# Nyström attention and two dense layers: heads paired by parity, landmark products as eight 64x32 tiles, second-layer blocks of 512, 512, 512, 384 and 384 tokens

## The chip, the cores and the metric

The kernel runs on one core of one Trainium2 chip. The metric is device time in microseconds (us), here the median of three timed runs. One further execution was recorded by the hardware profiler; all rows below come from it. The engines are PE (TensorE, matrix products; PEld is its weight load), DVE (VectorE), ACT (ScalarE), POOL (GpSimd) and SP (SyncE, which here issues the DMAs). Products accumulate in PSUM, which has eight banks of 128 partitions by 512 fp32 values.

## The reference

Attention with 32 landmarks a head (4 batches, 8 heads, 576 positions, head size 64), then two dense layers over the 2304 resulting tokens of width 512. Everything is fp32.

```python
# per batch and head; m = 32, S = 576, D = 64
q_lm, k_lm = means of q, k over S // m = 18 consecutive positions
A  = softmax(q @ k_lm.T / 8)      # 576 x 32
Bm = softmax(q_lm @ k_lm.T / 8)   # 32 x 32
C  = softmax(q_lm @ k.T / 8)      # 32 x 576
Z  = Bm.T / (norm1(Bm) * norminf(Bm) + 1e-6)
for _ in range(6): Z = 2 * Z - Z @ Bm @ Z
x = (A @ Z @ C @ v), heads side by side          # 2304 x 512
# layer 1: 512 -> 2048 -> 512
h = x @ moe_w_in;  y = (h * sigmoid(h)) @ moe_w_out
# layer 2: 512 -> 2048 -> 512
h = y @ moe2_w_in; out = (h * tanh(softplus(h))) @ moe2_w_out
```

## The kernel before

**Attention without x.** The kernel never forms x. For each batch it makes W = Z·C·v (32 landmarks by 64 values for each head) and multiplies it with the rows of the first layer's input weights that belong to the head: u = Wᵀ·w_in. Then h = uᵀ·Aᵀ, where Aᵀ lies with all 8 heads' landmarks on the partitions (`ath`, two groups of 128). Four heads make a unit (b, g), g = 0 or 1. W of a unit goes from a PSUM bank `wk` into a tile `wt`, block diagonal by a mask `own2`, so that one product with 128 rows serves two heads. `u_steps` (L518 to L549) makes u for a batch and a pair `jp` of the 16 column chunks of the hidden layer: eight fp32 matmuls of 128 rows by 64 columns of weights with 128 moving columns, all into one bank; each fp32 matmul runs as two instructions. There are 4 batches by 8 pairs, so 32 such groups. For batch 0 an ACT copy takes the bank to SBUF (L541). For the other batches ACT rounds it to a high part (L546) and DVE subtracts that for a low part (L548), and h is then three products (high·high, high·low, low·high) at L608, as are y and the second layer's `hh`.

**Layer 1.** Tokens go in blocks of 288. A step is one block and one of 16 chunks j of the hidden layer: 6 matmuls for h, SiLU on DVE, ACT and POOL, 12 matmuls for y. y goes to DRAM (`ysc`). Batches 0 and 1 begin in a prelude, in which a planner orders the streams of work (loads, transposes, landmark products, Newton steps, u, h) by listed costs and start delays; `ya` (L829) is batch 0's fp32 y. From then on a loop over steps runs, with the attention of the batch after next worked in between (`bg`). Attention and u of that loop share PSUM banks 5 and 7. In the last block of layer 1 the second layer's weights and inputs come in: each `w2r` tile is loaded by DMA and split in a high part on ACT (`wi2h`, `wh`, L602) and a low part on DVE or POOL (L603).

**Layer 2.** It is written in a fixed order by hand. `NB2` = 384 tokens make a block, 6 blocks, and 16 chunks j each, so 96 steps. A step is 12 matmuls for `hh` (L608, 384 columns each), mish on DVE and ACT over 128x384 tiles (L1025 to L1039), a low part on POOL (L1042), and, two steps later (`LAG2`), 9 matmuls into three banks `o` (L1098, 512 columns each). When a block's last step is accumulated, `out_block` (L1057) copies its three banks through ACT into `ot` tiles (three buffers, L1061) and SP issues the output DMAs (L1069). The `o` banks are five, taken by turns; `hh` has three.

Of the kernel before, what the change touches and what calls it, by code (L numbers as in the profile page):

```python
# [25 lines left out]
NB2 = 384  # L26
# [6 lines left out]
WASTE = 1.33  # L33
# [57 lines left out]
def nystrom_moe_kernel(ctx, tc, q, k, v, w1i, w1o, w2i, w2o, out):  # L91
# [32 lines left out]
    own2 = cp.tile([P, 2], F32, name="own2")  # L124
    blk = cp.tile([P, P], F32, name="blk")
    two = cp.tile([P, 1], F32, name="two")
    for t in (mask2, mask4, sel2, own2, blk):
        pool.memset(t, 0.0)
    pool.memset(two, 2.0)
    for h2 in range(2):  # L130
        pool.memset(mask2[64 * h2 : 64 * h2 + 64, h2 : h2 + 1], 1.0 / (G * 8.0))
        pool.memset(own2[64 * h2 : 64 * h2 + 64, h2 : h2 + 1], 1.0)
# [46 lines left out]
    def load_part(st, nm, p):  # L179
# [3 lines left out]
        h0 = 4 * g + 2 * p  # L183
        if nm != "v" and b in dve_tr:

            t = ap.tile([P, S // M, M], F32, tag=tag, bufs=2, name=f"{nm}{b}{g}{p}")
            for hf in range(2):
                for h2 in range(2):
                    for dh in range(2):
# [4 lines left out]
                            src[b, h0 + h2, hf * HB : (hf + 1) * HB, M * dh : M * dh + M].rearrange(  # L194
# [3 lines left out]
        else:  # L198
# [3 lines left out]
            for h2 in range(2):  # L202
                sp.dma_start(
                    t[:, h2] if apart else t[:, :, h2, :], src[b, h0 + h2].rearrange("(p c) d -> p c d", c=NC)
                )
# [205 lines left out]
    def attn_newton(bt):  # L411
# [27 lines left out]
        for i in range(n):  # L439
            for h2 in range(2):  # L440
                pe.matmul(wk[64 * h2 : 64 * h2 + 64, i, :P], rv[:, i, w:], bt["bb", i], start=True, stop=True)
        yield Step([("dve", 0.3)], (), ("wt", b, gs[-1]))
        for i, g in enumerate(gs):
            pl, tag = (wp, f"gt{g + 1}") if b == 0 else (ap, f"wt{g}")
            wt = pl.tile([P, 2, 2, M], F32, tag=tag, name=f"wt{b}{g}")
            dve.tensor_tensor(
                wt,
                wk[:, i, :P].rearrange("a (p h m) -> a p h m", p=2, h=2),
                own2[:, None, :, None].to_broadcast([P, 2, 2, M]),
                op=ALU.mult,  # L450
            )
            units[b, g]["wt"] = wt
# [65 lines left out]
    def u_steps(b, jp):  # L518

        deps = [("wt", b, 0), ("wt", b, 1)]  # L520
        if b == 0:
            deps += [("wc", 2 * jp), ("wc", 2 * jp + 1), ("ath", 0, 1)] + ([("u", 0, jp - 2)] if jp > 1 else [])
        elif b == 1:
            deps += [("y", 1, 2 * jp + 1)] + ([("u", 1, jp - 2)] if jp > 1 else [])
        yield Step([("pe", 0.9)], deps)
        ub = atbank(f"u{b}{jp}").rearrange("a (j g f) -> a j g f", j=2, g=2)
        for g in range(2):
            wt = units[b, g]["wt"]
            for jj in range(2):
                for p in range(2):  # L530
                    pe.matmul(  # L531
                        ub[64 * p : 64 * p + 64, jj, g],
                        wt[:, p].rearrange("a h m -> a (h m)"),
                        wc[2 * jp + jj][:, (2 * g + p) * P : (2 * g + p + 1) * P],
                        start=True,
                        stop=True,
                    )
        if b == 0:
            yield Step([("act", 0.6)], (), ("u", 0, jp))
            uw[jp] = wp.tile([P, 2, 2, P], F32, tag=f"u{jp}", name=f"uf{jp}")  # L540
            act.copy(uw[jp], ub)  # L541
            return
        yield Step([("act", 0.6)])
# [3 lines left out]
        yield Step([("dve", 0.7)], (), ("u", b, jp))  # L547
        dve.tensor_tensor(ul, ub, uh.bitcast(F32), op=ALU.subtract)  # L548
# [61 lines left out]
    wc = {}  # L610
    wout = {}

# [13 lines left out]
    def h0_matmuls(hb, j, hf):  # L626
        for g in range(2):
            pe.matmul(hb[:, :HB], uw[j // 2][:, j % 2, g], ath[0][:, g, hf * HB : (hf + 1) * HB], start=g == 0, stop=g == 1)  # L628

    def h1_matmuls(hb, b, j, hf):  # L630
        uh, ul = uw[j // 2]
        sl = slice(hf * HB, (hf + 1) * HB)
        for g in range(2):
            wh, wl = uh[:, j % 2, g], ul[:, j % 2, g]
# [213 lines left out]
    streams += [(head_load(*it), Banks(), 1.31) for it in order]  # L848
    streams += [(first_unit(0, 0), Banks(0, 1, 2), 0.38), (first_unit(0, 1), Banks(3, 4, 5), 0.05)]
    for g in range(2):  # L850
        streams += [(queries(units[0, g]), q01, (0.32, 0.25)[g])]
        for ti in range(2):
            streams += [(attn_transposes(units[0, g], ti, 3 * g + ti), Banks(), (1.35, 0.06)[g])]
    streams += [(u_steps(0, jp), Banks(6 + jp % 2), 0.38 + 0.05 * jp) for jp in range(NF // 2)]
    streams += [(h_stream(j, hf), Banks(), 0.59 + 0.01 * (2 * j + hf)) for j in range(NF) for hf in range(2)]
    streams += [(win_stream(j), Banks(), 1.08 + 0 * j) for j in range(NF)]
    streams += [(y_stream(), Banks(), 1.18)]
    streams += [(wout_stream(j), Banks(), 1.17 + 0.05 * j) for j in range(NF)]
    for g in range(2):
        streams += [(attn_transposes(units[1, g], ti, 4 + ti), Banks(), (0.75, 0.87)[g]) for ti in range(2)]  # L860
        streams += [(second_attention(g), a1, (0.67, 1.15)[g])]
        streams += [(attn_softmax(units[1, g]), a1, (1.36, 0.66)[g])]
    streams += [(u_steps(1, jp), Banks((3, 4)[jp % 2]), 1.24) for jp in range(NF // 2)]
    streams += [(wsplit_stream(j), Banks(), 2.0) for j in range(NF)]
# [302 lines left out]
```

## Time and profile before

| what | value |
|---|---|
| median of three runs | 896.05 us (895.35 to 901.98) |
| the profiled execution, its own time | 899.86 us |
| its span in the profile | 898.1 us |
| busy share of the span: PE / DVE / ACT / POOL | 96% / 73% / 53% / 33% |
| share of PE in the chain that ended last | 79% |
| PE busy in 0 to 100 us, 100 to 200, 300 to 400, 400 to 500 | 86.07, 96.22, 93.33, 95.69 us |
| PE busy in 200 to 300, 600 to 700, 700 to 800 us | 100.00 us each |

The prelude takes about the first 198 us, layer 1 lasts until about 487 us, layer 2 to the end. The profiled execution took 1.8 us more than its span shows and lies 3.8 us above the median. In a profile row "idle before, releaser" is how long the engine stood still just before the instruction and what set it free. Matmuls are pipelined: the spacing of their starts, not their durations, says what each costs. The granted TensorE clock (PEclk) is a share of full speed: 1.00 is 2.4 GHz and 0.50 is 1.2 GHz.

### The profile page before, as it was taken

How to read it: one execution, taken by the hardware profiler on the slowest of the kernel's cores; microseconds unless marked ns; L12 is line 12 of the kernel's file. 1: busy time of each engine (PE TensorE's matmuls, PEld its weight loads, DVE VectorE, ACT ScalarE, POOL GpSimd, SP SyncE). 2: the span in 40 equal slices, each digit the busy share in tenths (PEclk: the TensorE clock that was granted, in tenths of full speed). 3: DMA queues.
4: the chain of work that ended last, by engine and by line, in shares of the span. 5: the costliest groups of instructions: out<-in, count | busy, mean ns of one | idle time of the engine just before them, and what ended most of it. 6: DMA issues, size and time to landing. Idle time of an engine off the chain costs nothing.

```text
span 898.1 us, 15048 instructions
## 1 busy us (share of the span) xinstructions
PE 863.3 (96%) x5440; PEld 762.3 (85%) x5440; DVE 651.1 (73%) x1265; ACT 472.7 (53%) x1013; POOL 293.9 (33%) x334
## 2 busy tenths in 40 slices
PE   7799989999999998899999999999999999999997
PEld 5567767779998998899899889899999999999896
DVE  3878858676576968742364997787787787797776
ACT  3656546345344646653564555554554554555544
POOL 2211333015343545532433542242242242242221
PEclk8899989999999999999999999999999999999999
DMA  8645663433454576720562210110110110000000
GB/s 230 169 97 169 189 192 101 81 81 88 100 149 101 143 224 222 244 87 17 161 181 68 79 45 1 36 35 1 36 36 1 37 36 1 35 1 1 36 1 35
DMA packets 95354, 79.62 MB, mean 89 GB/s; under 512 B 52528, under 2 KB 80688, under 8 KB 95280
## 3 DMA queue, kind: packets, MB, share of 16 engines
q1 hardware_dynamic: 95280, 78.67, 30.6%
q8 instruction: 42, 0.69, 0.3%
q14 instruction: 32, 0.26, 0.1%
HBM read 60.82 MB, written 17.83 MB: 88 GB/s over the span
## 4 chain that ended last, share of the span: by engine, by line
PE 79%; DVE 8%; DMA 5%; ACT 3%; POOL 2%; issue 2%; SPq 1%; ACTq 0%; DVEq 0%; POOLq 0%
PE hh L608 21%; PE o L1098 20%; PE y L608 14%; PE h L608 7%; PE ya L829 5%; PE u L531 4%; PE ha L628 3%; DMA q<-in_q_dram 2%; PE nw L423 1%; DVE z L1036 1%; DMA w2r<-w2c 1%; DMA k<-in_k_dram 1%; PE cv L374 1%; POOL rawt L590 1%; PE c L307 1%
## 5 line engine op out<-in xcount | busy, mean ns | idle before, releaser
L1042 POOL TENSOR_TENSOR g<-z,g 128x384 fp32r<-128x384 f32 x94 | 96.0, 1022 | 256.0 <-ACT g L1039 253.6
L608 PE MATMUL y<-g,wh 128*128 128x288 f32 x768 | 162.4, 302 | 6.8 <-ACT g L659 2.9
L1098 PE MATMUL o<-wh,g 128*128 128x512 f32 x576 | 165.7, 395 | 2.9 <-ACT g L1039 1.9
L660 POOL TENSOR_TENSOR g<-g,g 128x288 fp32r<-128x288 f32 x96 | 82.4, 858 | 184.9 <-ACT g L659 143.0
L608 PEld LDWEIGHTS y<-g,wh 128*128 128x128 f32 x768 | 124.5, 190 | 12.0 <-ACT g L659 3.1
L608 PE MATMUL hh<-yl,wi2h 128*128 128x384 f32 x384 | 129.6, 337 | 0.0
L608 PE MATMUL hh<-yh,wi2h 128*128 128x384 f32 x384 | 129.2, 336 | 0.0
L608 PE MATMUL hh<-yh,wi2l 128*128 128x384 f32 x384 | 129.1, 336 | 0.0
L1098 PEld LDWEIGHTS o<-wh,g 128*128 128x128 f32 x576 | 106.0, 188 | 23.3 <-ACT g L1039 4.1
L1039 ACT CAST g<-z 128x384 fp32r<-128x384 f32 x96 | 49.3, 514 | 133.6 <-DVE z L1038 133.6
L608 PE MATMUL y<-g,wl 128*128 128x288 f32 x384 | 114.6, 298 | 0.0
L1025 DVE TENSOR_SCALAR e<-hh 128x384 f32<-128x384 f32 x96 | 53.5, 557 | 64.2 <-PE hh L608 63.9
L608 PE MATMUL h<-ath,uw 128*128 128x288 f32 x384 | 95.1, 302 | 0.0
L658 DVE SCALAR_TENSOR_TENSOR g<-th,h 128x288 f32<-128x288 f32 x96 | 43.0, 447 | 55.8 <-ACT th L657 54.3
L1098 PE MATMUL o<-wl,g 128*128 128x512 f32 x288 | 81.7, 391 | 0.0
L1026 ACT ACTIVATE e<-e 128x384 f32<-128x384 f32 x96 | 50.4, 525 | 51.4 <-DVE e L1025 51.2
L608 PEld LDWEIGHTS hh<-yl,wi2h 128*128 128x128 f32 x384 | 72.1, 188 | 3.7
L608 PEld LDWEIGHTS hh<-yh,wi2h 128*128 128x128 f32 x384 | 72.1, 188 | 3.7
L608 PEld LDWEIGHTS y<-g,wl 128*128 128x128 f32 x384 | 73.0, 190 | 0.0
L1036 DVE SCALAR_TENSOR_TENSOR z<-z,r 128x384 f32<-128x384 f32 x96 | 70.0, 729 | 3.3
L608 PEld LDWEIGHTS hh<-yh,wi2l 128*128 128x128 f32 x384 | 72.1, 188 | 0.0
L608 PEld LDWEIGHTS h<-ath,uw 128*128 128x128 f32 x384 | 68.1, 191 | 3.6 <-issue 3.0
(165 smaller groups left out, 1631.7 us busy)
## 6 DMA issues: line engine op xcount, KB each, us to landing
rawi<-in_moe_w_in_dram SPq DMA_DIRECT2D x16, 512.0 KB, 5.6
rawo<-in_moe_w_out_dram SPq DMA_DIRECT2D x16, 512.0 KB, 3.6
rawt<-in_moe_w_in_dram SPq DMA_DIRECT2D x16, 512.0 KB, 4.7
w2c<-ct SPq DMA_DIRECT2D x32, 256.0 KB, 2.6
rawt<-in_moe_w_out_dram SPq DMA_DIRECT2D x16, 512.0 KB, 3.8
w2r<-w2c SPq DMA_DIRECT2D x32, 256.0 KB, 2.8
v<-in_v_dram SPq DMA_DIRECT2D x32, 144.0 KB, 3.1
ysc<-yo SPq DMA_DIRECT2D x32, 144.0 KB, 1.9
```

What stands on the lines that cost most here:

```text
L531: pe.matmul(ub[64 * p : 64 * p + 64, jj, g], wt[:, p].rearrange("a h m -> a (h m)"), wc[2 * jp + jj][:, (2 * g + p) * P : (2 * g + p + 1) ...
L608: pe.matmul(o, a, b_, start=first and i == 0, stop=last and i == n - 1)
L628: pe.matmul(hb[:, :HB], uw[j // 2][:, j % 2, g], ath[0][:, g, hf * HB : (hf + 1) * HB], start=g == 0, stop=g == 1)
L658: dve.scalar_tensor_tensor(g2, th, 1.0, hb[:, :HB], op0=ALU.add, op1=ALU.mult)
L660: eng.tensor_tensor(gl, g2, gh.bitcast(F32), op=ALU.subtract)
L829: pe.matmul(yb[hf, m][:, :HB], wof[j][:, m * P : (m + 1) * P], gst[j // 2][:, j % 2, hf], start=j == 0, stop=j == NF - 1,)
L1025: dve.tensor_scalar(e, h, 20.0, None, op0=ALU.min)
L1026: ins = act.activation(e, e, AF.Exp)
L1036: dve.scalar_tensor_tensor(z, z, -2.0, r, op0=ALU.add, op1=ALU.mult)
L1039: act.copy(gh, z)
L1042: eng.tensor_tensor(gl, z, gh.bitcast(F32), op=ALU.subtract)
L1098: pe.matmul(obank[i][c], a[:, c * P : (c + 1) * P], w, start=j == 0 and k == 0, stop=j == NF - 1 and k == 2,)
```

## The change

**Heads.** A unit g now holds the heads 2(2p + h2) + g, the even or the odd ones. W of unit g lies only in partitions 64g to 64g + 63 of its `wt` ([128, 4, 32]), as a plain copy; the mask is gone, and `wk` is one matmul a unit instead of two. u for a pair jp is again eight matmuls, but of 64 rows by 32 columns of weights with 256 moving columns, and it fills half of two banks, one for each unit. So ACT makes two copies of 128x256 where it made one of 128x512, and DVE two subtractions of 128x256. Each u takes two banks: in the prelude 6 and 7 (batch 0), or 3 and 7 and 4 and 5 by turns (batch 1), in the layer-1 loop both 5 and 7. Batch 0's u(jp) now waits for u(jp-1) where it waited for u(jp-2).

**Blocks.** Layer 2 has five blocks, three of 512 tokens with four output chunks and two of 384 with three, so 80 steps: 48 with 12 `hh` matmuls and 12 `o` matmuls of 512 columns each, and 32 as before. `ot` has two buffers instead of three. The low parts of the second layer's input weights for j >= 2 take SBUF that holds u of batch 3 (tags g0 to g6), so they wait for its last h matmuls; j < 2 have tiles of their own.

**Order of the prelude.** Start delays and costs of the planner's streams are other numbers (ten lines such as the one shown), and `WASTE`, a factor on its time, is 1.14 instead of 1.33.

```diff
-NB2 = 384
+NB2 = (512, 512, 512, 384, 384)
@@ first_unit: W into wt
-        for i in range(n):
-            for h2 in range(2):
-                pe.matmul(wk[64 * h2 : 64 * h2 + 64, i, :P], rv[:, i, w:], bt["bb", i], start=True, stop=True)
+        for i, g in enumerate(gs):
+            pe.matmul(wk[64 * g : 64 * g + 64, i, :P], rv[:, i, w:], bt["bb", i], start=True, stop=True)
-            wt = pl.tile([P, 2, 2, M], F32, tag=tag, name=f"wt{b}{g}")
-            dve.tensor_tensor(
...
+            wt = pl.tile([P, 4, M], F32, tag=tag, name=f"wt{b}{g}")
+            sl = slice(64 * g, 64 * g + 64)
+            dve.tensor_copy(wt[sl].rearrange("a h m -> a (h m)"), wk[sl, i, :P])
@@ u_steps
-        ub = atbank(f"u{b}{jp}").rearrange("a (j g f) -> a j g f", j=2, g=2)
-        for g in range(2):
-            wt = units[b, g]["wt"]
-            for jj in range(2):
-                for p in range(2):
-                    pe.matmul(
-                        ub[64 * p : 64 * p + 64, jj, g],
-                        wt[:, p].rearrange("a h m -> a (h m)"),
-                        wc[2 * jp + jj][:, (2 * g + p) * P : (2 * g + p + 1) * P],
...
+        ub = [atbank(f"u{b}{jp}{g}") for g in range(2)]
+        for h in range(4):
+            for g in range(2):
+                sl = slice(64 * g, 64 * g + 64)
+                pe.matmul(
+                    ub[g][32 * h : 32 * h + 32, : 2 * P].rearrange("a (j f) -> a j f", j=2),
+                    units[b, g]["wt"][sl, h],
+                    wcp[jp][sl, :, h * P : (h + 1) * P],
...
-        act.copy(uh, ub)
+        for g in range(2):
+            act.copy(uh[:, g].rearrange("a j f -> a (j f)"), ub[g][:, : 2 * P])
-        dve.tensor_tensor(ul, ub, uh.bitcast(F32), op=ALU.subtract)
+        for g in range(2):
+            dve.tensor_tensor(
+                ul[:, g].rearrange("a j f -> a (j f)"),
...
@@ the planner's streams
-    streams += [(u_steps(0, jp), Banks(6 + jp % 2), 0.38 + 0.05 * jp) for jp in range(NF // 2)]
+    streams += [(u_steps(0, jp), Banks(6, 7), 0.07 + 0.05 * jp) for jp in range(NF // 2)]
@@ second-layer weights
-                    if j < 11:
+                    if j < 2:
                         lo = pl.tile([P, ND, P], F32R, tag=f"lo{j}", name=f"wi2l{j}")
                     else:
-                        lo = wp.tile([P, ND, P], F32R, tag=f"g{j - 11}", name=f"wi2l{j}")
+                        if j % 2 == 0:
+                            los = wp.tile([P, 2, ND, P], F32R, tag=f"g{j // 2 - 1}", name=f"wi2l{j}")
+                        lo = los[:, j % 2]
@@ out_block and out_matmuls
-        for c in range(NCH):
-            ot = m2.tile([P, DM], F32, tag="ot", bufs=3, name=f"ot{i}_{c}")
+        for c in range(NB2[i] // P):
+            ot = m2.tile([P, DM], F32, tag="ot", bufs=2, name=f"ot{i}_{c}")
-            obank[i] = [bank((NCH * i + c + 4) % 5, f"o{i}_{c}") for c in range(NCH)]
+            obank[i] = [bank((sum(NB2[:i]) // P + c + 4) % 5, f"o{i}_{c}") for c in range(chunks)]
```

So the four-chunk blocks use the `o` banks 4, 0, 1, 2, then 3, 4, 0, 1, then 2, 3, 4, 0, and the three-chunk blocks 1, 2, 3 and 4, 0, 1.

On PE, in the layer-1 loop where batch 2's first u stands between h and y of a step, the kernel before has these rows (u is the product, wc the weights of layer 1, wt is W):

```order
L608 MATMUL h_3077<-atl_1242,uw_7_1808 128x288
L608 MATMUL h_3077<-ath_1241,uw_7_1808 128x288
L531 MATMUL u_3091<-wc_652,wt_2878 64x128 x2
L531 MATMUL u_3091<-wc_676,wt_2878 64x128 x2
L531 MATMUL u_3091<-wc_652,wt_2880 64x128 x2
L531 MATMUL u_3091<-wc_676,wt_2880 64x128 x2
L608 MATMUL y_0_2498<-g_288_2980,wh_13_1759 128x288 x2
```

The changed kernel has, at the same place:

```order
L610 MATMUL h_3105<-atl_1214,uw_7_1825 128x288
L610 MATMUL h_3105<-ath_1213,uw_7_1825 128x288
L525 MATMUL u_3119<-wc_603,wt_2900 32x256
L525 MATMUL u_3120<-wc_603,wt_2902 32x256
L525 MATMUL u_3119<-wc_603,wt_2900 32x256
L525 MATMUL u_3120<-wc_603,wt_2902 32x256
```

Four more u rows follow by turns, then y. There are still eight u matmuls, now by turns for the upper and the lower 64 rows and into two banks, u_3119 and u_3120; the place between h and y is the same.

On PE in the prelude, among batch 0's y products `ya`, stand the transposes of batch 1's second half of q and k, right behind one another before:

```order
L829 MATMUL ya_1188<-gs_873,wl_6_1255 128x288
L829 MATMUL ya_1190<-gs_873,wl_6_1255 128x288
L246 MATMUL tr_1344<-ident,q_1317 128x96 x3
L246 MATMUL tr_1349<-ident,k_1323 128x96 x3
L829 MATMUL ya_1182<-gs_932,wl_8_1293 128x288
L829 MATMUL ya_1184<-gs_932,wl_8_1293 128x288
```

In the changed kernel the first three transposes of that q stand behind as many `ya` matmuls (40) as before, but those of k come 15 `ya` later; these rows run from the second transposes of q to the first of k:

```order
L245 MATMUL tr_1349<-ident,q_1311 128x96 x3
L836 MATMUL ya_1183<-gs_938,wl_8_1315 128x288
L836 MATMUL ya_1185<-gs_938,wl_8_1315 128x288
L836 MATMUL ya_1187<-gs_938,wl_8_1315 128x288
L836 MATMUL ya_1189<-gs_938,wl_8_1315 128x288
L836 MATMUL ya_1191<-gs_938,wl_8_1315 128x288
L836 MATMUL ya_1183<-gs_1010,wl_10_1345 128x288
L836 MATMUL ya_1185<-gs_1010,wl_10_1345 128x288
L836 MATMUL ya_1187<-gs_1010,wl_10_1345 128x288
L836 MATMUL ya_1189<-gs_1010,wl_10_1345 128x288
L836 MATMUL ya_1191<-gs_1010,wl_10_1345 128x288
L245 MATMUL tr_1387<-ident,k_1363 128x96 x3
```

On ACT in the last block of layer 1, before (th and g are a step's SiLU, wi2h the high part of a second-layer weight tile whose DMA is w2r):

```order
L602 CAST wi2h_5261<-w2r_2_5215 128x512
L659 CAST g_288_5026<-g_5028 128x288
L602 CAST wi2h_5295<-w2r_3_5253 128x512
L657 ACTIVATE th_5062<-h_5054 128x288
L659 CAST g_288_5061<-g_5063 128x288
L602 CAST wi2h_5331<-w2r_4_5259 128x512
L657 ACTIVATE th_5095<-h_5087 128x288
L602 CAST wi2h_5367<-w2r_5_5293 128x512
L659 CAST g_288_5094<-g_5096 128x288
L657 ACTIVATE th_5135<-h_5127 128x288
L602 CAST wi2h_5407<-w2r_6_5329 128x512
L659 CAST g_288_5134<-g_5136 128x288
```

In the changed kernel:

```order
L604 CAST wi2h_5328<-w2r_2_5283 128x512
L667 CAST g_288_5094<-g_5096 128x288
L604 CAST wi2h_5328<-w2r_3_5321 128x512
L665 ACTIVATE th_5130<-h_5122 128x288
L667 CAST g_288_5129<-g_5131 128x288
L665 ACTIVATE th_5163<-h_5155 128x288
L667 CAST g_288_5162<-g_5164 128x288
L665 ACTIVATE th_5203<-h_5195 128x288
L667 CAST g_288_5202<-g_5204 128x288
L665 ACTIVATE th_5233<-h_5225 128x288
L688 ACTIVATE yo_1_5258<-y_1_4662 128x288
L667 CAST g_288_5232<-g_5234 128x288
```

There the conversions pause after the fourth (wi2h from w2r_3) for five steps and then come two to a step for eleven steps, where before they went on without a pause at about 1.25 a step.

## Rows read from the trace of the kernel before

**Rows 1.** The page: engines, then shares of the chain that ended last.

```profile
PE 863.3 (96%) x5440; PEld 762.3 (85%) x5440; DVE 651.1 (73%) x1265; ACT 472.7 (53%) x1013; POOL 293.9 (33%) x334
...
PE 79%; DVE 8%; DMA 5%; ACT 3%; POOL 2%; issue 2%; SPq 1%; ACTq 0%; DVEq 0%; POOLq 0%
```

**Rows 2.** Timeline, one u in layer 1: start, duration, instruction, idle before.

```profile
297.73 0.29 PE L608 MATMUL h<-ath,uw 128*128 128x288 f32 x1
297.95 1.09 PE L531 MATMUL u<-wc,wt 128*64 128x128 f32 x16
298.98 0.53 PE L608 MATMUL y<-g,wh 128*128 128x288 f32 x2
```

**Rows 3.** Timeline of the 10 to 20 ns in which that u begins.

```profile
297.95 0.14 PEld L531 LDWEIGHTS u<-wc,wt 128*64 128x64 f32 x2 [0.17 <-issue]
297.95 0.33 PE L531 MATMUL u<-wc,wt 128*64 128x128 f32 x2
```

**Rows 4.** Timeline, fp32 matmuls of 288 columns in a row, and what follows.

```profile
111.70 5.01 PE L829 MATMUL ya<-gs,wl 128*128 128x288 f32 x20
116.55 0.41 PE L246 MATMUL tr<-ident,q 96*128 96x96 f32 x3
```

**Rows 5.** Tile u: count, ns min/median/max, first and last start, shape.

```profile
L546 ACT CAST uw<-u x24: 578/582/588, 174.4 to 425.5; 128x512 fp32r<-128x512 f32 x24
L548 DVE TENSOR_TENSOR uw<-u,uw x24: 647/692/692, 175.0 to 426.1; 128x512 fp32r<-128x512 f32 x24
```

**Rows 6.** The chain that ended last: start, length, what; layer 2.

```profile
704.37 2.09 PE hh L608 x12
706.46 2.06 PE o L1098 x9
```

**Rows 7.** The page, costliest groups: busy, mean ns, idle before and releaser.

```profile
L1025 DVE TENSOR_SCALAR e<-hh 128x384 f32<-128x384 f32 x96 | 53.5, 557 | 64.2 <-PE hh L608 63.9
```

**Rows 8.** Timeline, end of the first layer-2 block (its output).

```profile
564.28 1.56 ACT L1061 ACTIVATE ot<-o 128x512 f32<-128x512 f32 x3
...
564.89 3.12 SPq L1069 DMA_DIRECT2D out_dram<-ot  x6
564.92 0.19 PEld L1098 LDWEIGHTS o<-wh,g 128*128 128x128 f32 x1 [0.30 <-ACT ot L1061]
```

**Rows 9.** DMA issues: count, KB each, median us from issue to landing.

```profile
out_dram<-ot SPq DMA_DIRECT2D x9, 256.0 KB, 2.2
```

**Rows 10.** Timeline, PE, two starts after a wait in layer 1.

```profile
348.92 0.50 PE L608 MATMUL y<-g,wh 128*128 128x288 f32 x2 [2.61 <-DVE yo L682]
...
364.40 0.69 PE L423 MATMUL nw<-rv,rb 128*128 128x96 f32 x4 [2.28 <-DVE rv L435]
```

**Rows 11.** Busy time by stretch; third figure from the end: granted clock.

```profile
128.00:135.00 7.00, 6.39 (x20) 4.88 (x21) 1.00 (x2) 0.70 (x2) 1.93 (x3) 0.52 0.52 196
350.00:353.00 3.00, 3.00 (x14) 2.96 (x14) 2.05 (x4) 2.22 (x6) 1.89 (x3) 0.50 0.91 219
363.00:368.00 5.00, 3.60 (x28) 3.60 (x29) 3.51 (x8) 3.68 (x10) 1.64 (x3) 1.00 0.73 243
452.00:456.00 4.00, 4.00 (x21) 4.00 (x20) 2.48 (x5) 1.88 (x4) 1.05 (x1) 0.57 0.88 274
```

**Rows 12.** Timeline, the last output chunks.

```profile
893.69 1.51 SPq L1069 DMA_DIRECT2D out_dram<-ot  x3
894.00 0.39 ACT L1066 ACTIVATE ot<-o 128x256 f32<-128x256 f32 x1 [0.33 <-PE o L1098]
```

**Rows 13.** Timeline, last block of layer 1: ACT, then PE.

```profile
448.67 0.62 ACT L602 CAST wi2h<-w2r 128x512 fp32r<-128x512 f32 x1 [1.94 <-DMA w2r<-w2c]
450.89 0.51 PE L608 MATMUL y<-g,wh 128*128 128x288 f32 x2 [2.94 <-ACT g L659]
```

**Rows 14.** Timeline, PE, transposes in the prelude that waited for loads.

```profile
126.86 0.44 PE L246 MATMUL tr<-ident,q 96*128 96x96 f32 x3 [1.47 <-DMA q<-in_q_dram]
128.61 0.72 PE L246 MATMUL tr<-ident,k 96*128 96x96 f32 x3 [1.32 <-DMA k<-in_k_dram]
```

More of the change, by code (lines that the diff above doesn't have):

```diff
@@ L182, in load_part @@
         src = {"q": q, "k": k, "v": v}[nm]
-        h0 = 4 * g + 2 * p
+        heads = [2 * (2 * p + h2) + g for h2 in range(2)]
         if nm != "v" and b in dve_tr:
@@ L203, in load_part @@
                 sp.dma_start(
-                    t[:, h2] if apart else t[:, :, h2, :], src[b, h0 + h2].rearrange("(p c) d -> p c d", c=NC)
+                    t[:, h2] if apart else t[:, :, h2, :], src[b, heads[h2]].rearrange("(p c) d -> p c d", c=NC)
                 )
@@ L548, in u_steps @@
-        dve.tensor_tensor(ul, ub, uh.bitcast(F32), op=ALU.subtract)
+        for g in range(2):
+            act.copy(uh[:, g].rearrange("a j f -> a (j f)"), ub[g][:, : 2 * P])
+        yield Step([("dve", 0.8)], (), ("u", b, jp))
+        for g in range(2):
+            dve.tensor_tensor(
+                ul[:, g].rearrange("a j f -> a (j f)"),
+                ub[g][:, : 2 * P],
+                uh[:, g].bitcast(F32).rearrange("a j f -> a (j f)"),
+                op=ALU.subtract,
+            )
@@ L627, in h0_matmuls @@
         for g in range(2):
-            pe.matmul(hb[:, :HB], uw[j // 2][:, j % 2, g], ath[0][:, g, hf * HB : (hf + 1) * HB], start=g == 0, stop=g == 1)
+            pe.matmul(hb[:, :HB], uw[j // 2][:, g, j % 2], ath[0][:, g, hf * HB : (hf + 1) * HB], start=g == 0, stop=g == 1)
     def h1_matmuls(hb, b, j, hf):
@@ L863, in nystrom_moe_kernel @@
-    streams += [(u_steps(1, jp), Banks((3, 4)[jp % 2]), 1.24) for jp in range(NF // 2)]
-    streams += [(wsplit_stream(j), Banks(), 2.0) for j in range(NF)]
+        streams += [(attn_transposes(units[1, g], ti, 4 + ti), Banks(), (0.75, 1.26)[g]) for ti in range(2)]
+        streams += [(second_attention(g), a1, (0.58, 1.08)[g])]
+        streams += [(attn_softmax(units[1, g]), a1, (1.36, 0.11)[g])]
+    streams += [(u_steps(1, jp), Banks(*((3, 7), (4, 5))[jp % 2]), 1.24) for jp in range(NF // 2)]
@@ L865, in nystrom_moe_kernel @@
+    streams += [(wsplit_stream(j), Banks(), 2.04) for j in range(NF)]
     attn2 = attn_batch(2)
@@ L952, in gtiles @@
     def gtiles(t, n):
-        gt_ = wp.tile([P, 2, n], F32R, tag=f"gt{t % 3}", name=f"g{t}_{n}")
-        return gt_[:, 0], gt_[:, 1]
+        if "tail" not in late:
+            gt_ = wp.tile([P, 2, HB], F32R, tag=f"gt{t % 3}", name=f"g{t}_{n}")
+        elif t % 3 == 2:
+            gt_ = wp.tile([P, 2, BIG], F32R, tag="g7", name=f"g{t}_{n}")
+        else:
+            gt_ = late["tail"].tile([P, 2, BIG], F32R, tag=f"gz{t % 3}", bufs=1, name=f"g{t}_{n}")
+        return gt_[:, 0, :n], gt_[:, 1, :n]
     def emit_y(t):
@@ L1067, in out_block @@
                 dve.tensor_scalar(ot[:, h:], obank[i][c][:, h:], -1.0, None, op0=ALU.mult)
-            for r0, r1, rows in out_rows(i * NB2 + c * P):
+            for r0, r1, rows in out_rows(sum(NB2[:i]) + c * P):
                 sp.dma_start(rows, ot[r0:r1])
@@ L1090, in out_matmuls @@
         wh, wl = wout2[j]
+        chunks = NB2[i] // P
         if j == 0:
-            obank[i] = [bank((NCH * i + c + 4) % 5, f"o{i}_{c}") for c in range(NCH)]
-        order = [(c, k) for k in range(3) for c in range(NCH)]
+            obank[i] = [bank((sum(NB2[:i]) // P + c + 4) % 5, f"o{i}_{c}") for c in range(chunks)]
+        order = [(c, k) for k in range(3) for c in range(chunks)]
         if t == len(steps) - 1:
```

96 lines of the change are left out of this document (47 added, 49 removed).

## The prediction

> **What bounds the kernel now.** I read the engines' busy shares first, then the chain that ended last, then the stretches, then single places. PE is busy for 863.3 of 898.1 us and makes 79% of the chain [rows 1]: wherever PE is full, time goes by what PE issues, and a saving elsewhere shows only where PE waits. PE is full from 200 to 300 us, where layer 1 runs beside the attention of batch 2, and from 600 to 800 us in layer 2; its idle time lies in the prelude, at four or five holes of 1.3 to 3 us in layer 1, and at the very end. In layer 2 the reader should see a step as 2.09 us of `hh` and 2.06 us of `o`, back to back [rows 6], while DVE stands still for 64.2 us in 96 steps until `hh` ends [rows 7]. So a change is worth what it takes from or adds to PE's queue, plus what it does to those holes.
>
> **u in tiles.** One u now: the last h begins at 297.73 and would be followed after its own spacing (0.13, by the 0.229 of 512 columns below), at 297.86; y begins at 298.98 [rows 2]. So u costs about 1.1 us. Two of its 16 instructions start within the same 0.02 us [rows 3], that is, the two column halves run side by side, in eight rounds. An fp32 instruction of 288 columns takes (116.55 - 111.70)/20 = 0.2425 us, so 0.842 ns a column [rows 4], 0.108 us for 128 columns; eight rounds are 0.86 us, and the rest is start and change of shape. After, there are again 16 instructions, of 256 columns, 0.216 us each. What they cost depends on how many run side by side, which no row shows for 64 rows of weights or for four column groups:
> - all eight tiles together, each in two passes: 0.43 us, a gain of 0.43 a u and 32 x 0.43 = 13.8 us;
> - the two row halves by turns: 0.86, no gain;
> - tiles two at a time, the second pass of one pair beside the first of the next: five rounds, 1.08, a loss of 0.22 a u and 7 us;
> - two at a time and nothing else: eight rounds, 1.73, a loss of 0.87 a u and 28 us; one after another would be 3.46.
>
> I take the first, since the nearest row shows two instructions on different parts of the array start together and the weight load of the second beside the first [rows 3]; the others stay as bounds. The Trainium skill ("TensorE: Matmul & The Clock Gate", Part 3, The mechanism) says that a weight load overlaps running matmuls only where the row group differs. By that the four tiles of one row half could not run together, and the sum would be the fourth case, +28 instead of -13.8. The row does not bear it out: the two loads there share all rows. The same page's table of packed tiles (Measured speedup) speaks for the first case.
>
> The halved `wk` matmuls save under 1 us in all, behind the Newton steps on which PE waits for DVE; I count nothing.
>
> **Emptying u.** One copy of 582 ns and one subtraction of 692 ns on 512 columns [rows 5] become two of each on 256. A 256-column copy on ACT takes 0.39 [rows 12], which on DVE by the same ratio is 0.46: 1.70 instead of 1.27 us until a bank is free, and both banks are held where one was left to the attention. If each of the 16 u of the layer-1 loop made PE wait for the whole difference it would cost 16 x 0.43 = 6.9 us; if the y matmuls between two u (12 or more) hide it, nothing. I take +2. In batch 0 u(jp) now waits for u(jp-1), but they stand 2 to 4 us apart there, more than the 0.8 us of two copies: nothing.
>
> **Blocks of 512.** A step of 384 costs 2.09 + 2.06 = 4.15 us [rows 6]. A matmul of 512 columns costs 2.06/9 = 0.229, so a step of 512 is 24 x 0.229 = 5.49. 64 steps at 4.15 are 265.6 us, 48 at 5.49 are 263.5: -2. DVE's six operations a step, like the one of 557 ns [rows 7], grow by at most a third, to some 4.5 us together, under 5.49: PE remains the bound.
>
> **Output of a block.** Now ACT empties three banks in 1.56 us, and a new `o` waits only 0.30 for its bank [rows 8]. With two `ot` buffers the third copy waits until the first chunk has landed: issue 0.61 us after the copies begin [rows 8], 2.2 us of DMA [rows 9], a few tenths of queue: 2.8 to 3.2. It ends 0.52 later, at 3.6. Blocks 1 and 2 take their fourth `o` bank from that third chunk, and `o` goes round all four banks before it repeats, so PE's fourth `o`, due at about 1.3, waits until 3.6. SP and the DMAs stay in order behind it, and ACT's e and g of the next steps stand behind the copies. I take +2.4 at each of the two changes between four-chunk blocks, +0.7 in all at the two later ones, where the new block does not use the late bank: +5.5. The bounds are +2 (a landing in 1.9 us and ACT work behind it covered) and +8.
>
> A stall of that size may also slow the clock: after PE stood still for 2.61 us it was granted 0.50 from 350 to 353 us, after 2.28 us it kept 1.00 [rows 10, 11]. Half clock over 3 us costs 1.5. My 2.4 lies between; I take one of the two: +1.5 (0 to 3).
>
> **The end.** The third chunk of the last block is copied at 894.00 and its buffer is now the first chunk's, issued at 893.69 [rows 12] and landed 2.0 to 2.2 us later: +1.8.
>
> **The hole in layer 1.** ACT waits 1.94 us for a second-layer weight, SiLU is queued behind it, and PE stands still for 2.94 us [rows 13], then has 0.57 of the clock for 4 us [rows 11], 1.7 us more: 4.6 in all. After, the conversions pause there and come later, two a step: ACT has SiLU's two operations of about 0.4 each (by the 0.39 of 256 columns [rows 12]) and two conversions of 0.62 [rows 13], 2.1 us, in a step of 18 matmuls of 288 columns, 18 x 0.229 x 288/512 = 2.3; the loads are 0.5 MB a step, some 225 GB/s, where 274 was reached [rows 11]. That fits narrowly, so part of it may come back: -3 (-4.6 to +1).
>
> **The prelude.** The k transposes that waited 1.32 us [rows 14] now stand 15 `ya` later, at 0.485 us each some 7 us, so that wait goes; q's 1.47 may stay. The two holes left PE at 0.52 of the clock for 7 us [rows 11], 3.4 us lost. I take -2 (-6 to +3, for the rest of the new order, in which C comes ahead of the query products and the Newton steps of the two units are staggered).
>
> **Sum.** -13.8 + 2 - 2 + 5.5 + 1.5 + 1.8 - 3 - 2 = -10.0: span 888.1, execution 899.86 - 10.0 = 889.9. That execution lay 3.8 above the median of 896.05, so the forecast is 886.1 us.
>
> **Rivals.**
> - Slower: pairs. The eight tiles run two at a time with overlap of one pass, u costs 1.08, so 20.7 us more than forecast: 906.8. It decides from about 1.0 us of columns a u. For it: only pairs are ever seen together in this trace. Against: nothing in the row shows that pairs are the limit, since only two tiles existed. The fourth case of the list is its worse end, 886.1 + 13.8 + 27.8 = 927.7.
> - No gain from the tiles: the row halves take turns, u costs what it did, 899.9. The new waits then eat what the blocks and holes give.
> - Waits: u comes out as forecast, but banks and buffers cost their upper bounds: +3 for u's banks, +1.5 for the second half clock at a block's end, +3 because the hole in layer 1 stays: 893.6. For it: ACT and DVE gain nothing by tiles, and the copies grow. The Trainium skill says this of tiling ("TensorEngine Tiling (Array Packing)", PSUM Bottleneck and PSUM Pressure): TensorE gets faster but emptying PSUM does not, and different row tiles need different banks.
> - More: the hole goes whole (-1.6), both waits for loads and their half clock go (-4), u's banks never bind (-2), the clock holds at the block ends (-1.5): 877.
>
> **Numbers.** Forecast case (880 to 891) 0.48, waits 0.19, no gain 0.11, pairs or worse 0.12, more 0.10. A measurement here can tell about 1% from no change: faster is under 887.1, slower over 905.0. Of the forecast case 0.40 lies under 887.1, with the case "more" 0.50 faster; 0.38 within 1% (the rest of the forecast, waits, no gain); 0.12 slower. The range for 8 in 10 is 875 to 903: it reaches from "more" to "no gain" and leaves out the pairs and half of the far ends.
>
> **What would show it.** Right: the u row has 16 instructions in about 0.6 us instead of 1.09, with several starting in the same 0.02 us; layer-2 steps of 5.5 us in the chain; ACT's third `ot` copy idle some 1 to 2 us for a DMA, and PE's `o` waiting for `ot` about 2.4 us at the first two block ends but not at the last two; the last copy waiting about 1.8 us for the first chunk's DMA; no wait of ACT for w2r near the last block's fifth step. Wrong: u of 1.3 us or more (pairs); PE waiting for ACT or DVE's u before attention's products (waits); block ends without a PE wait, because `out` lands sooner than its row; or new holes in the prelude, which the order alone cannot show.

## The result and the profile after

The changed kernel took 890.38 us (median of five runs, 887.95 to 890.5) where the kernel before took 896.41 in the same set: ratio 0.9908, interval 0.9879 to 0.9937. So it is faster by 0.9%, less than the 1% taken here as the least that a measurement tells plainly. The forecast was 886.1 in a range of 875 to 903. The profiled execution took 889.39 us, 1.0 below the median; its span is 887.6, 10.5 shorter than that of the kernel before, whose profiled execution lay above its median. By the two medians the gain is 6.0 us, by the ratio 8. Everything below that compares spans or stretches rests on one profiled execution of each kernel.

The page of the changed kernel (engines, and shares of the chain that ended last), which answers to [rows 1]:

```profile
PE 848.9 (96%) x5232; PEld 714.9 (81%) x5232; DVE 633.5 (71%) x1193; ACT 465.1 (52%) x977; POOL 288.1 (32%) x311
...
PE 73%; DVE 8%; DMA 6%; ACT 4%; issue 4%; POOL 3%; SPq 1%; ACTq 0%; DVEq 0%; POOLq 0%
```

PE is busy 14.4 us less, but its share of the chain fell from 79% to 73%: some of what PE no longer does became waiting. Two starts, taken from the timelines of both kernels, say where. First the kernel before (the first h of batch 1, at the end of the prelude, and the first `hh` of layer 2):

```profile
193.01 0.40 PE L608 MATMUL h<-ath,uw 128*128 128x288 f32 x1
...
485.26 0.34 PE L608 MATMUL hh<-yh,wi2h 128*128 128x384 f32 x1
```

Then the changed kernel:

```profile
179.76 0.40 PE L610 MATMUL h<-ath,uw 128*128 128x288 f32 x1
...
465.93 0.39 PE L610 MATMUL hh<-yh,wi2h 128*128 128x512 f32 x1
```

Up to the end of the prelude 13.2 us are gained, in layer 1 another 6.1, and layer 2 then takes 887.6 - 465.9 = 421.7 us instead of 898.1 - 485.3 = 412.8: 8.9 are given back. The sum is, but for rounding, the 10.5 by which the spans differ. Such a split is good to a few us only: in the kernels below that share the changed prelude and u the first h of batch 1 stands between 178.6 and 186.0.

**u.** One u in layer 1 (timeline of PE), which answers to [rows 2]:

```profile
386.96 0.29 PE L610 MATMUL h<-ath,uw 128*128 128x288 f32 x1
387.18 0.66 PE L525 MATMUL u<-wc,wt 64*32 64x256 f32 x16
387.77 0.53 PE L610 MATMUL y<-g,wh 128*128 128x288 f32 x2
```

From u's start to y's it is 0.59 us, before 1.03: a gain of 0.44 a u. Not every u gains that: of the 32, four in the changed kernel take 0.9 to 1.5 us, the first two of them at half clock, and all 32 together take 21.1 us where they took 32.7. Two of the 16 that stood ahead of that first h now stand behind it.

**Block ends.** The changed kernel at the end of the first block of layer 2 (ACT's timeline), which answers to [rows 8]:

```profile
567.30 1.07 ACT L1080 ACTIVATE ot<-o 128x512 f32<-128x512 f32 x2
571.05 1.32 ACT L1080 ACTIVATE ot<-o 128x512 f32<-128x512 f32 x2 [2.69 <-DMA out_dram<-ot]
```

and PE's first `o` behind it, and the same place one block later:

```profile
571.70 0.79 PE L1118 MATMUL o<-wh,g 128*128 128x512 f32 x1 [2.79 <-ACT ot L1080]
...
664.81 0.50 PE L1118 MATMUL o<-wh,g 128*128 128x512 f32 x1 [2.64 <-ACT ot L1080]
```

The third copy starts 3.75 us after the first, when the first chunk's DMA has freed its buffer, and PE's fourth `o` waits for that copy. The granted clock behind the two waits (busy time by stretch; third figure from the end):

```profile
571.70:577.00 5.30, 5.30 (x13) 4.14 (x14) 1.38 (x2) 2.98 (x5) 1.29 (x1) 0.50 0.32 99
664.80:670.00 5.20, 5.19 (x22) 4.24 (x23) 1.38 (x3) 2.98 (x5) 1.30 (x1) 1.00 0.39 102
```

After the longer wait PE was granted 0.50 and its matmuls ran at half rate until about 577.7, which lost 3.0 us; after the shorter it kept 1.00. At the end of the kernel the last copy of ACT, against [rows 12]:

```profile
881.06 0.60 ACT L1080 ACTIVATE ot<-o 128x512 f32<-128x512 f32 x1 [1.51 <-PE o L1118]
883.83 0.38 ACT L1085 ACTIVATE ot<-o 128x256 f32<-128x256 f32 x1 [2.18 <-DMA out_dram<-ot]
```

**The banks of u.** What PE waited for, by line (total, times, longest):

```profile
PE o L1118 <- ACT ot L1080: 5.4, 2, 2.8
...
PE cp L357 <- DVE uw L545: 2.2, 1, 2.2
...
PE h L610 <- DVE uw L545: 1.1, 1, 1.1
```

The 2.2 us stand at 297.02, where attention's transposes `cp` follow a u and find both banks held. That u had given way to y at 292.98. Its copies on ACT and its subtractions on DVE are these:

```profile
295.22 0.64 ACT L542 CAST uw<-u 128x256 fp32r<-128x256 f32 x2
...
296.55 0.74 DVE L545 TENSOR_TENSOR uw<-u,uw 128x256 fp32r<-128x256 f32 x2
```

They took 0.64 and 0.74 us, but ACT took them up 2.2 us after u and DVE 1.3 us after that: both engines were first busy with, or waiting for, the splitting of weights and SiLU. So the banks were held for some 4 us, and most of that was standing in line, not copying. Behind the wait the clock fell:

```profile
297.80:301.20 3.40, 3.40 (x16) 3.40 (x15) 0.45 (x1) 1.16 (x3) 0.80 (x1) 0.50 0.43 139
```

That lost 1.7 us more. The 1.1 us of `h` are a wait for u's low part itself, not for a bank.

### The profile page after: what moved, and what is told of

Read it like the earlier page. It is cut to its first block, busy times and chain, and to the rows that moved or that the text cites. A ratio compares the mean times of both kernels' runs of the same rounds, so it can differ in the third digit from the quotient of the medians.

```text
span 887.6 us, 14453 instructions
## 1 busy us (share of the span) xinstructions
PE 848.9 (96%) x5232; PEld 714.9 (81%) x5232; DVE 633.5 (71%) x1193; ACT 465.1 (52%) x977; POOL 288.1 (32%) x311
## 4 chain that ended last, share of the span: by engine, by line
PE 73%; DVE 8%; DMA 6%; ACT 4%; issue 4%; POOL 3%; SPq 1%; ACTq 0%; DVEq 0%; POOLq 0%
PE hh L610 21%; PE o L1118 21%; PE y L610 11%; PE h L610 5%; PE ya L836 5%; PE ha L636 4%; PE u L525 2%; POOL g L668 2%; DMA q<-in_q_dram 2%; DMA rawt<-in_moe_w_out_dram 1%; DMA out_dram<-ot 1%; PE nw L422 1%; PE cv L373 1%; POOL rawt L592 1%; DVE rawt L597 1%
## 5 line engine op out<-in xcount | busy, mean ns | idle before, releaser
L1061 POOL TENSOR_TENSOR g<-z,g 128x512 fp32r<-128x512 f32 (+1 forms) x78 | 92.9, 1191 | 266.7 <-ACT g L1058 260.3
L610 PE MATMUL hh<-yh,wi2h 128*128 128x512 f32 (+1 forms) x320 | 119.3, 373 | 0.0
L610 PE MATMUL hh<-yh,wi2l 128*128 128x512 f32 (+1 forms) x320 | 119.2, 373 | 0.0
L610 PE MATMUL hh<-yl,wi2h 128*128 128x512 f32 (+1 forms) x320 | 119.1, 372 | 0.0
L1044 DVE TENSOR_SCALAR e<-hh 128x512 f32<-128x512 f32 (+1 forms) x80 | 51.0, 637 | 86.9 <-PE hh L610 86.8
L1058 ACT CAST g<-z 128x512 fp32r<-128x512 f32 (+1 forms) x80 | 46.2, 577 | 121.3 <-DVE z L1057 118.5
L1045 ACT ACTIVATE e<-e 128x512 f32<-128x512 f32 (+1 forms) x80 | 47.1, 588 | 71.1 <-DVE e L1044 70.8
L610 PEld LDWEIGHTS hh<-yh,wi2h 128*128 128x128 f32 x320 | 60.4, 189 | 9.6
L610 PEld LDWEIGHTS hh<-yl,wi2h 128*128 128x128 f32 x320 | 60.3, 189 | 9.5
L836 PE MATMUL ya<-gs,wl 128*128 128x288 f32 x256 | 68.0, 411 | 0.0
```

Source lines behind the costliest of these rows:

```text
L610: pe.matmul(o, a, b_, start=first and i == 0, stop=last and i == n - 1)
L836: pe.matmul(yb[hf, m][:, :HB], wof[j][:, m * P : (m + 1) * P], gst[j // 2][:, j % 2, hf], start=j == 0, stop=j == NF - 1,)
L1044: dve.tensor_scalar(e, h, 20.0, None, op0=ALU.min)
L1045: ins = act.activation(e, e, AF.Exp)
L1058: act.copy(gh, z)
L1061: eng.tensor_tensor(gl, z, gh.bitcast(F32), op=ALU.subtract)
```

## The experiments

All are edits of the changed kernel. Ratios are to the kernel before.

**Three output buffers.**

```diff
-            ot = m2.tile([P, DM], F32, tag="ot", bufs=2, name=f"ot{i}_{c}")
+            ot = m2.tile([P, DM], F32, tag="ot", bufs=3, name=f"ot{i}_{c}")
```

> The changed kernel with three ot buffers instead of two, nothing else. Theory: PE's waits of 2.79 and 2.64 us at the first two block ends come from the third output copy waiting for the first chunk's DMA; the half clock after the first of them (6.07 us at 0.50, 3.0 lost) and the 1.9 us at the end hang on the same buffer. Then all of it goes: 2.8 + 2.6 + 3.0 + 1.9 = 10.3, about 880 us, and PE never waits for ot. The fourth copy will still wait for a DMA, but the next block's first step does not use its bank. Rival: four copies in a row on ACT, which delay the mish of the next steps, make the wait; then a wait of about 2 us stays, now on g, and the time is 885 or more.

Measured: 880.84 us (879.29 to 885.33), ratio 0.9807 (0.9784 to 0.983). The timelines of ACT and of PE at the first block's end:

```profile
569.10 1.55 ACT L1080 ACTIVATE ot<-o 128x512 f32<-128x512 f32 x3
572.90 0.60 ACT L1080 ACTIVATE ot<-o 128x512 f32<-128x512 f32 x1 [2.25 <-DMA out_dram<-ot]
```

```profile
569.69 1.51 PE L1118 MATMUL o<-wh,g 128*128 128x512 f32 x4
571.04 1.09 PE L1118 MATMUL o<-wl,g 128*128 128x512 f32 x4
```

ACT still waits 2.25 us, now for the fourth copy, and e and g of the next steps still stand behind it, but PE's `o` runs through and the clock stays at 1.00. So it was the bank of the third chunk and not ACT's delay that stopped PE. Layer 2 takes 411.4 us here, 1.4 less than before the change and 10.3 less than in the changed kernel. By the medians one buffer of 2 KB a partition is worth 9.5 us, where about 10 were expected, and this kernel is faster than both.

**Blocks as before.**

```diff
-NB2 = (512, 512, 512, 384, 384)
+NB2 = (384, 384, 384, 384, 384, 384)
```

(and three `ot` buffers, as before)

> The changed kernel with the blocks of before (six of 384 tokens, three ot buffers): heads, u and the prelude's order alone. Theory: the part up to layer 2 took 19.3 us less than before and layer 2 8.9 us more, and these add; without the blocks the time is 890.4 - 8.9 = 881 us or a little less. Rival: the later start of layer-2 weights takes some of the 19.3 back in layer 2; then it is 885 or more.

Measured: 885.64 us (880.54 to 889.51), ratio 0.9844 (0.9816 to 0.9873). That is the rival's time, not the 881 of the theory. The part up to layer 2 keeps its gain (first `hh` at 468.4 of a span of 883.7), but layer 2 takes 415.3 us with the blocks that took 412.8. The rival's mechanism, late weights, is not what the trace shows: in layer 2 PE waits no more than before. All its matmuls are spaced a little wider (in the kernel before a step was 2.09 and 2.06 us [rows 6]):

```profile
701.31 2.10 PE hh L610 x12
703.41 2.08 PE o L1118 x9
```

That is 0.03 us a step and 2.9 in 96 steps, about the 2.5 us by which layer 2 is longer; the last two experiments suggest that it goes with where the tiles lie. Against the kernel with three buffers and 512-token blocks layer 2 is 3.9 us slower, but only 1.4 of this can be put down to the blocks when the kernel before is the measure.

**The blocks alone.** The heads, `wk`, `wt` and `u_steps` of before and all numbers of the planner of before were put back; blocks, buffers and places of the second layer's weights stayed.

```diff
-        heads = [2 * (2 * p + h2) + g for h2 in range(2)]
+        heads = [4 * g + 2 * p + h2 for h2 in range(2)]
-        ub = [atbank(f"u{b}{jp}{g}") for g in range(2)]
+        ub = atbank(f"u{b}{jp}").rearrange("a (j g f) -> a j g f", j=2, g=2)
...
-WASTE = 1.14
+WASTE = 1.33
```

> The changed kernel with heads, u, wt and all numbers of the planner as before: the blocks, the ot buffers and the places of the second layer's weights alone. Theory: layer 2 loses 8.9 us as in the changed kernel, and layer 1's hole near the second-layer weights goes, 4.6: about 896.4 + 8.9 - 4.6 = 901 us. If the hole went for another reason: 905.

Measured: 900.43 us (898.01 to 905.46), ratio 1.0022 (1.0006 to 1.0039). With two buffers the blocks by themselves cost 2 us. The time is the 901 of the theory, but layer 2 lost 5.1 us here (417.9) and not 8.9. In its trace PE waits 2.15 and 2.67 us for `ot`, and the hole in layer 1 near the second-layer weights [rows 13] is gone, here as in the kernel with the old blocks. So it went neither by u nor by the blocks; of the parts of the change that leaves the later places of the weights.

**The old order of the prelude.** Heads, u and blocks as changed, all delays and WASTE as before.

```diff
-WASTE = 1.14
+WASTE = 1.33
-    streams += [(head_load(*it), Banks(), 1.27) for it in order]
+    streams += [(head_load(*it), Banks(), 1.31) for it in order]
...
```

> The changed kernel with all delays and WASTE of the planner as before, heads, u and blocks as changed. Theory: the new order of the prelude is worth what went beyond u there. Up to the first h of batch 1 13.2 us were gained, of which 16 u give 6.9; so some 5 us are given back and the time is about 895. Rival: the planner comes to nearly the same without the numbers, since shorter u alone shift the loads: 890 to 891.

Measured: 896.69 us (893.89 to 899.63), ratio 0.9982 (0.9968 to 0.9997). So the rival falls: the numbers are worth some 6 to 7 us. The first 200 us by busy time in this kernel:

```profile
0.00:100.00 100.00, 82.60 (x658) 56.94 (x659) 69.05 (x171) 55.87 (x143) 20.56 (x49) 0.91 0.62 166
100.00:200.00 100.00, 93.38 (x546) 66.33 (x545) 72.18 (x145) 49.53 (x111) 22.03 (x24) 0.98 0.47 125
```

and the same in the changed kernel:

```profile
0.00:100.00 100.00, 86.45 (x670) 61.73 (x670) 72.98 (x176) 59.44 (x152) 20.61 (x49) 0.88 0.62 171
100.00:200.00 100.00, 96.78 (x602) 72.17 (x603) 76.94 (x153) 50.27 (x112) 27.89 (x30) 1.00 0.48 137
```

With the old order the first h of batch 1 stands at 192.15, 0.9 us earlier than before the change, though the 16 u in front of it take 6.2 us less:

```profile
192.15 0.40 PE L610 MATMUL h<-ath,uw 128*128 128x288 f32 x1
```

PE idles instead: what it waited for, by line, in this kernel (three of the lines, over the whole span):

```profile
PE tr L245 <- DMA q<-in_q_dram: 4.3, 2, 2.9
PE cp L357 <- DVE uw L545: 3.9, 1, 3.9
...
PE tr L245 <- DMA k<-in_k_dram: 1.6, 1, 1.6
```

From 60 us to that h PE waits 10.8 us here, 5.2 before and 2.1 in the changed kernel. The transposes do come before their loads, but that is the smaller part: the waits for q and k in this stretch are 5.9 us where they were 4.4, and the rest that is new are waits for DVE and ACT, such as 1.9 us in the Newton steps (`nw`) and 1.1 before `cv`. The 3.9 us of `cp` stand in layer 1, at 308.68, and are u's banks again, with 0.57 of the clock for the 6 us behind them. Shorter u alone was worth 3.7 us (against the blocks alone), shorter u with the order made for it 10.

**u's tiles in another order.**

```diff
-        for h in range(4):
-            for g in range(2):
+        for g in range(2):
+            for h in range(4):
```

> The changed kernel with u's eight tiles in another order: the four tiles of the upper 64 rows first, then the four of the lower. Theory: all eight run side by side whatever their order, u from start to the next matmul stays 0.60 us. Rival: a weight load overlaps only matmuls of the other row half, as the Trainium skill (TensorE: Matmul & The Clock Gate, Part 3, The mechanism) says; then the order by turns hid the loads and this one does not, and u takes 0.8 us or more.

Measured, one run: 885.0 us; u in PE's timeline:

```profile
175.88 0.66 PE L525 MATMUL u<-wc,wt 64*32 64x256 f32 x16
176.47 1.72 PE L836 MATMUL ya<-gs,wl 128*128 128x288 f32 x6
```

0.59 us, as in the changed kernel. The weight loads of the same u:

```profile
175.88 0.18 PEld L525 LDWEIGHTS u<-wc,wt 64*32 64x32 f32 x16 [0.39 <-DVE uw L545]
```

All sixteen end within 0.18 us, while the first matmuls still run. Here, too, a weight load of a row half runs beside matmuls of that half; the rule that the expectation cites from the Trainium skill ("TensorE: Matmul & The Clock Gate", Part 3, The mechanism) does not hold for column groups in this case. From the one time nothing follows.

**u on one row half.**

```diff
-                    units[b, g]["wt"][sl, h],
-                    wcp[jp][sl, :, h * P : (h + 1) * P],
+                    units[b, 0]["wt"][0:64, h],
+                    wcp[jp][0:64, :, h * P : (h + 1) * P],
```

> The changed kernel with all eight tiles of u on the upper 64 rows, two on each 32 columns (the lower half's weights and inputs are left out of u). Theory: the row halves of the changed kernel run together and that is half of its gain; on one half the tiles of one column group must take turns, four rounds of 0.216 us, so u takes about 1.03 us as before the change, 0.43 more than now, and the kernel some 10 us longer, about 900. Rival: the row halves took turns anyway, then u stays 0.60.

Measured, one run: 903.42 us; u:

```profile
177.12 1.09 PE L525 MATMUL u<-wc,wt 64*32 64x256 f32 x16
178.14 1.72 PE L836 MATMUL ya<-gs,wl 128*128 128x288 f32 x6
```

1.02 us, as expected: with all tiles on one row half u costs what it did before the change. So in the changed kernel the two row halves run together, and that doubles the rate. The kernel before had the columns' share already, as two halves of 64 columns; what the change gained is the rows' share. This kernel leaves the lower half's weights and inputs out of u and serves for its timing alone. Its time is 13 us above the median of the changed kernel, where some 10 were expected and 32 u of 0.43 are 13.8: in the order made for short u nearly the whole of u counts.

**u at the end of a step.** With three buffers, the calls of `u_all` moved behind `emit_y` and the pieces of attention:

> The changed kernel with three ot buffers, and in the layer-1 loop u is issued at the end of a step, behind the pieces of attention, instead of ahead of them. Theory: PE's wait of 2.2 to 2.4 us for DVE's u, near 298 us, comes from attention's transposes that follow u at once and find both banks held; with a step between, it goes: about 878.5 us against 880.8 with three buffers alone. Rival: another piece of attention then finds the banks held, or h finds u late: 881 or more.

Measured: 884.92 us (882.15 to 889.54), ratio 0.9871 (0.9844 to 0.9897). The rival was right. PE's timeline, and the stretch behind (the profiled execution was the slowest of the six):

```profile
304.18 1.08 PE L525 MATMUL u<-wc,wt 64*32 64x256 f32 x8 [2.67 <-ACT ct L359]
```

```profile
304.00:310.00 6.00, 5.82 (x29) 4.96 (x29) 3.16 (x6) 1.61 (x5) 2.27 (x3) 0.50 0.22 63
```

Now u waits for the transposes' bank instead of the transposes for u's, and the clock falls to 0.50 behind it. Two users of the same two banks meet in either order.

**512-token blocks in other places.** With three buffers:

```diff
-NB2 = (512, 512, 512, 384, 384)
+NB2 = (512, 512, 384, 512, 384)
```

> The changed kernel with three ot buffers and blocks of 512, 512, 384, 512 and 384 tokens. In the traces of all kernels with 512-token blocks the second block's matmuls start 0.227 us apart and those of the first and third 0.231 to 0.234, which makes the third 1.8 us longer. If that goes with the y buffers (the even blocks have one pair, the odd ones another), the fourth block is now also at 0.227 and the time 1.8 us shorter, about 879. If it goes with the place in the kernel or with what runs beside it, nothing changes: 880.8.

Measured: 880.71 us (877.62 to 884.57), ratio 0.9831 (0.9805 to 0.9857). The spacing did move: the fourth block's matmuls now start 0.227 us apart. But of the 1.8 us expected from it the trace shows 0.4, layer 2 taking 411.0 us instead of 411.4, and the time cannot tell so little.

**The y tiles moved by 32 bytes.** In the built program the y tiles of the odd blocks begin at a multiple of 64 bytes in their partition, as nearly all weights of the second layer do, those of the even blocks 32 bytes beyond one. Two kernels with three buffers, one that moves the even blocks' tiles, one that moves the odd ones':

```diff
-                        lo = pl.tile([P, ND, P], F32R, tag=f"lo{j}", name=f"wi2l{j}")
+                        lo = pl.tile([P, ND * P + 8 * (j == 0)], F32R, tag=f"lo{j}", name=f"wi2l{j}")[:, : ND * P]
```

> The kernel with three ot buffers and 32 bytes more in one tile, by which the tiles of the second layer's y of the even blocks (and the raw and yo tiles beside them) move down by 32 bytes and begin at a multiple of 64 bytes in their partition, as those of the odd blocks did already. Theory: where the moving operand begins at 32 beyond a multiple of 64, a matmul starts 0.231 to 0.234 us after the one before it, else 0.227; then blocks 1 and 3 fall to 0.227 too, 1.8 us for each 512-token block and about 1 for the last, some 4 to 5 us in all: about 876. Rival: it is the place in memory or what runs beside it: 880.8 and no change in the spacing.

Measured: 878.35 us (877.1 to 881.64), ratio 0.9801 (0.9773 to 0.9828).

```diff
-            gt_ = late["tail"].tile([P, 2, BIG], F32R, tag=f"gz{t % 3}", bufs=1, name=f"g{t}_{n}")
+            gt_ = late["tail"].tile([P, 2 * BIG + 8 * (t % 3)], F32R, tag=f"gz{t % 3}", bufs=1, name=f"g{t}_{n}")
```

> The kernel with three ot buffers and the y tiles of the odd blocks moved up by 32 bytes, so that all y tiles begin at 32 beyond a multiple of 64. By the theory of the 64 bytes the second block's matmuls go from 0.227 to 0.231 or more and the time rises by some 3 us to 884. By the rival nothing changes: 880.8. (In the kernel with the blocks alone, the second block was at 0.227 with its y tiles so placed, which speaks for the rival.)

Measured: 880.39 us (879.07 to 882.35), ratio 0.9814 (0.9788 to 0.984). This is the rival's time and not the 884 of the theory, though the spacing moved as the theory said; layer 2 takes 412.4 us, 1.1 more than with three buffers alone.

The chain in the second block with three buffers alone (y at a multiple of 64), then with the odd blocks moved off it:

```profile
602.96 2.72 PE o L1118 x12
605.68 2.72 PE hh L610 x12
```

```profile
600.77 2.76 PE o L1119 x12
603.52 2.80 PE hh L610 x12
```

and in the third block with three buffers alone (y 32 bytes off), then with the even blocks moved onto a multiple:

```profile
683.07 2.81 PE hh L610 x12
```

```profile
681.39 2.76 PE hh L610 x12
```

So moving y changes the spacing of `hh`, by 0.08 and 0.05 us in 12 matmuls, 1.3 and 0.8 us in a 512-token block. It is not the whole of it. In the second block `o`, which does not read y, slowed by 0.04 with the same edit. On a multiple of 64 the third block stays at 2.76 where the second is at 2.72. And in the kernel with the blocks alone, where y lies 32 bytes off in all blocks, the second and the third block are as fast as here with y on a multiple:

```profile
608.18 2.72 PE hh L609 x12
...
694.91 2.76 PE hh L609 x12
```

There the second layer's weights were 32 bytes off too, so it may be that both must lie alike, which would fit these kernels. That was not tried by itself and stays open. Layer 2 took 409.4 us with the even blocks moved (411.4 without), 2.0 less, not the 4 to 5 expected; the medians agree with that, and their intervals overlap. Its median is the lowest of this study, but the kernels with three buffers alone, with shuffled blocks and with the odd blocks moved cannot be told from it by their times.

## Why the prediction was right, and where its terms were off

The measured 890.38 us lies in the range, 4.3 above the forecast. The mechanisms were in the main those of the forecast, with u's banks as the exception. 10.0 us of gain were forecast in the span and 10.5 came, but that close agreement is in part luck: the medians differ by 6.0, the two profiled executions lie on opposite sides of theirs, and inside the sum some terms were off by as much as they cancelled.

- **u, -13.8.** Right in a u that nothing disturbs, 0.44 instead of 0.43, and all eight tiles run together, as u on one row half and u's tiles in another order show. The rivals of pairs and of row halves by turns fell. All 32 u together gained 11.5. What the step left out is that with the old order a shorter u in the prelude turns into waiting, for loads and more for DVE and ACT: by itself it was worth 3.7 us.
- **Prelude, -2.** Mis-sized. Up to the first h of batch 1 13.2 us were gained; u there, 16 before and 14 after, accounts for 6.9, and 6.3 remain; the old order gives back 6 to 7. From 60 us to that h the waits fell from 5.2 to 2.1 us, and the half clock of [rows 11], 3.4 us, did not come. The two holes that the forecast names gave most of this: the wait for k went, q's 1.47 became 1.26 and the clock stayed at 1.00, 4.9 in all by the forecast's own rows, of which it counted 2. A third wait for q, 1.59 at 62.92, went too. And it should have been asked what the old order does with shorter u: without the new one most of the saving in the prelude is lost.
- **u's banks, +2.** Too small, and for another reason than the forecast's: waits of 2.2, 1.1 and 0.4 us and 1.7 of lost clock, 5.4, inside the bounds of 0 to 6.9. The forecast charged the longer copies, 0.43 a u. The one large wait came from copies that stood in line on ACT and DVE behind other work, and the 1.1 is not a bank at all.
- **Blocks, -2.** Right in direction: 1.4 less in layer 2 with three buffers, though that also holds what the new places of the tiles cost. A 512-token step takes 2.81 + 2.76 = 5.57 us in the third block and 5.44 in the second; the forecast's 5.49 lies between.
- **Block ends, +5.5, and the clock, +1.5.** 5.4 at the first two and nothing at the later two, so the sum came out because the two waits were longer than 2.4 by what the later two did not cost. The clock fell behind one of two, as taken, but for 6 us, 3.0 lost instead of 1.5.
- **The end, +1.8.** The last copy came 2.77 us behind the first where it was 0.93: 1.84.
- **Hole, -3.** It went whole, 4.6. ACT still waits for w2r in the last block, once for long:

```profile
423.17 0.62 ACT L604 CAST wi2h<-w2r 128x512 fp32r<-128x512 f32 x1 [2.37 <-DMA w2r<-w2c]
```

From 405 to 465 us, though, PE has no wait over 0.34 us. Earlier in layer 1, three waits of 0.8 to 1.1 us came between 334 and 340, for y's copies and g, where the kernel before had one of 2.61 and half clock behind it [rows 10, 11]. Layer 1 as a whole gained 6.1, of which u, 16 before and 18 after, accounts for 4.6.
- **The rival of waits** was said to take upper bounds, but its +3, +1.5 and +3 are less than the bounds that the terms themselves state (+4.9 over the 2 for u's banks, +2.5 and +1.5 at the block ends, +4 for the hole). At those it would have lain above 893.6.

## What to carry to other kernels

A saving on the bounding engine counts only where the engine's next work is ready: in a prelude ordered by hand or by a planner the order must be made anew for the shorter operation; here more than half of the gain lay there. When blocks grow, count the buffers behind them again: here one output buffer too few cost 9 to 10 us, through a DMA that freed the buffer, a copy that freed a bank, and the clock. Small products of 64 rows by 32 columns can share the array eight at a time, but here their products then lay in two banks, and what mattered was when ACT and DVE came to empty them, not how long that took.

## What was not expected of the hardware

- Two waits of nearly the same length were followed by different clocks: 2.79 us by half clock for 6 us, 2.64 us by none. The longer cost about twice itself. The length alone does not decide: in the traces here waits of PE of 2.13, 2.19, 2.25, 2.63, 2.66 and 2.67 us were followed by some 3 us or more at half clock, others of 2.13, 2.15, 2.42, 2.64, 2.65 and 2.68 us by none.
- fp32r matmuls of 512 columns started 0.227 or 0.234 us apart, and moving the moving tile between a multiple of 64 bytes and 32 beyond it, with the weights at a multiple, moved 0.227 to 0.233 in one block and 0.234 to 0.231 in another; the rest of the difference (0.227 against 0.231 at equal places) is unexplained.
- Eight fp32 tiles of 64 rows by 32 columns, two instructions each, took 0.59 us in all until the next matmul; two to each column group on one row half took 1.02.
